# One ring of 20 buffers for ScalarE's copies, four plain column blocks in the second token block, and transposes and loads one slot earlier

## The chip, the cores and the metric

The kernel runs on one core of one Trainium2 chip. The metric is device time in microseconds (us) of that core. TensorE (PE) multiplies, VectorE (DVE) adds and takes maxima, ScalarE (ACT) mostly copies accumulators out of PSUM, GpSimd (POOL) does a few products in SBUF, and SyncE (SP) issues nearly all DMAs, one behind the other.

## The reference

A retention layer (causal attention with a decay in place of the softmax, 8 batches of 576 tokens, 8 heads of 64) is followed by a feed-forward layer whose hidden value is the maximum of three products:

```python
scores = (1 / sqrt(64)) * (q @ k^T)                 # q, k, v: (8, 8, 576, 64)
ret = scores * Dmat                                 # Dmat: gamma_h ** (i - j) for i >= j, else 0
x = (ret @ v), heads side by side                   # (4608, 512)
h = max(x @ w1, x @ w2, x @ w3)                     # w: (512, 768)
out = h @ w_out                                     # (4608, 512), float32
```

The feed-forward weights arrive in 64 bits and are converted to float32 on the chip.

## The kernel before

**Tiles.** The 4608 tokens are 36 chunks of 128 tokens; four chunks make a token block t (t = 0 to 8, 512 tokens). The 768 hidden columns are six column blocks fb of 128. The attention of a chunk is `load` (DMA), `transposes`, `decay_values` (POOL), `scores` (PE), a mask product (DVE), and, for two chunks at once, `values` (PE), whose result DVE writes to `xT`. From chunk 7 on a chunk's q and k for the transposes come in 32x32 blocks: `load` then issues 16 DMAs for `qraw`, 16 for `kxraw`, and one or two each for `kraw` and `vraw`, all on SP's queue, and the transposes are two DVE instructions (`kT`, `qT`). The buffers `qraw` and `kxraw` are two each, so that a load of chunk g + 2 waits for the transposes of chunk g.

**The order.** `ffn(t)` is a generator that hands back control 12 times per token block: nine times within the products of the hidden columns and three times within the down projection. Before each of these 12 slots the program runs the list that `steps(t + 1)` has for it: the attention of the next token block, laid out by hand. So the instructions of each engine stand in program order, and each engine works them off in that order. Small DVE jobs (sums of weights, sums of x, transposes) are put into `urgent` or `chores` and taken from there by `chore()` between matmuls; `soon(step)` puts a step into `urgent`, or runs it at once while `t = 0`, before `spread` is set.

**Hidden columns.** In t = 0 each (fb, i) is done plainly by `up_plain`: four matmuls of 128x128 by 128x512, and then ACT copies the first product (L631) or DVE takes the maximum (L630). From t = 1 on `up` does a column block with 20 products of 128x128 by 128x256 in five chains A to E, which accumulate in PSUM; sums of x (`X_SUMS`, tiles `s`) and of weights (`W_SUMS`, tiles `w` and `n`, called `weight_sums(fp)` for a pair fp of column blocks) are their operands. At certain steps of a chain `after(step)` has ACT copy the chain's present value to SBUF (L573), and DVE combines the copies (`join`, L569); the last joins give the two halves of `h`, `lo` and `hi`. The next matmul of the same chain waits for that copy. In t = 1 the column blocks 2 and 3 are still done plainly. The tiles that hold the copies exist once each: `of_a` and `of_b` with four slices each, and `a1`, `c1`, `d1`, `a7`, `b6`. PSUM has two buffers `ps_x` (chains A and B, in turn) and two `ps_y` (chains E, C, D, in turn).

**Down projection.** `downs_plain` in t = 0: four accumulators of 128x512, in the order ps_x, ps_y, ps_x, ps_y; ACT copies each to `osb` (L620), of which there are two, and SP stores it (L621). From t = 1 on `downs` does seven products per half (L419), with ACT copies (`kept`), DVE sums (`total`, L442) into the same two `osb` buffers, and stores on SP (L437).

Of the kernel before, what the change touches and what calls it, by code (L numbers as in the profile page):

```python
# [51 lines left out]
BY_PE = 7  # L52
AHEAD = 3
FILL = 224

X_SUMS = """s19 = a12 + a14, s15 = s19 - a22, s3 = a22 - a12, s10 = s3 - a13, s13 = a12 + a13, s20 = s10 + a23,
            s14 = a24 - s15, s11 = s20 + a24, s11 = a21 - s11, s7 = s11 - s13, s6 = s19 + s7,
# [5 lines left out]

PRODUCTS = """E a11 b12, E a14 b42, B s15 n5, A a22 b21, C s3 b23, B s19 b41, A s10 b32, C a13 b31, B s6 n2, A s13 b22,
              C a11 b11, B s14 n1, A s11 n4, D s7 b43, B a23 n6, A s20 b33, D s16 b13, B a21 n3, A a21 n8, A a24 n7"""
X_SUMS, W_SUMS = ([x.split() for x in text.split(",")] for text in (X_SUMS, W_SUMS))
PRODUCTS = [x.split() for x in PRODUCTS.split(",")]
WAHEAD = 6
# [3 lines left out]
def kernel(  # L72
# [30 lines left out]
    stp = ctx.enter_context(tc.tile_pool(name="stp", bufs=4))  # L103
    xpool = ctx.enter_context(tc.tile_pool(name="xpool", bufs=2))
    hpool = ctx.enter_context(tc.tile_pool(name="hpool", bufs=1))
    ppool = ctx.enter_context(tc.tile_pool(name="ppool", bufs=2))
    opool = ctx.enter_context(tc.tile_pool(name="opool", bufs=2))
    while_converting = ExitStack()
    wraw = while_converting.enter_context(tc.tile_pool(name="wraw", bufs=WAHEAD))
# [286 lines left out]
    def downs(t, h):  # L396

        def raw_hidden(r, e):
            return lambda fp: h[:, 2 * fp + e, NH * r:NH * (r + 1)]

        def summed(n):
            return lambda fp: late["S"][n][:, fp, :]

        NM = NH // P
        banks = {}
        last = t == N // NT - 1
        hS = {1: raw_hidden(0, 0), 2: raw_hidden(0, 1), 3: summed(4), 4: raw_hidden(1, 1),
              5: summed(1), 6: summed(2), 7: summed(3)}

        def bank(pool, tag, name):  # L410
            b = pool.tile([P, NM, DM // 2], FP32, tag=tag, name=name)
            both = [b[:, m, :] for m in range(NM)]
            banks[id(both)] = b
            return both

        def product(n, out, first, blocks=range(NM)):
            for fp in range(NF // 2):
                for m in blocks:
                    nc.tensor.matmul(out[m], lhsT=hS[n](fp)[:, m * P:(m + 1) * P], rhs=late["T"][n][:, fp, :],  # L419
                                     start=first and fp == 0 and (m == 0 or last and out is x),  # L420
                                     stop=fp == NF // 2 - 1, skip_group_check=True)

        def kept(name, src):
            c = ppool.tile([P, 4, NH], FP32, tag=name, name=name, bufs=1)
            if last:
                for m in range(NM):
                    nc.scalar.copy(c[:, m], src[m])
            else:
                nc.scalar.copy(c[:, 0:NM].rearrange("p m d -> p (m d)"), joined(src))
            return c  # L430

        def joined(both):
            return banks[id(both)][:].rearrange("p m d -> p (m d)")

        def store(r, c, osb, blocks=slice(None)):
            block = out[t * NT + r * NH:t * NT + (r + 1) * NH, c * (DM // 2):(c + 1) * (DM // 2)]
            nc.sync.dma_start(block.rearrange("(m p) d -> p m d", p=P)[:, blocks], osb[:, blocks])  # L437

        def total(r, c, src, others):
            osb = opool.tile([P, NM, DM // 2], FP32, tag="osb", name="osb")  # L440
            if id(src) in banks:
                nc.vector.tensor_tensor(osb[:].rearrange("p m d -> p (m d)"), joined(src),  # L442
                                        others[:, 0:NM].rearrange("p m d -> p (m d)"), op=ALU.add)
            else:
                for m in range(NM):
                    nc.vector.tensor_tensor(osb[:, m, :], src[m], others[:, m], op=ALU.add)
# [7 lines left out]
        p1 = kept("of_a", x)  # L454
# [6 lines left out]
        u2 = kept("of_a", x)  # L461
        yield
        z = bank(ps_y, "y", "dz")
        product(7, z, True)
        p7 = kept("of_b", z)
        yield
        product(5, x, False)
        total(1, 1, x, p7)
        yield
        product(4, z, False)  # L470
        total(1, 0, z, u2)
        yield
        osb = opool.tile([P, NM, DM // 2], FP32, tag="osb", name="osb")
        for blocks in ([[m] for m in range(NM)] if last else [range(NM)]):
            product(3, x, False, blocks)
            for m in blocks:
                nc.scalar.copy(osb[:, m, :], x[m])
            store(0, 1, osb, slice(blocks[0], blocks[-1] + 1))
        yield
# [75 lines left out]
    def up(t, h, fb):  # L555
# [2 lines left out]


        lo, hi = h[:, fb, 0:NH], h[:, fb, NH:NT]  # L560
        of_a = ppool.tile([P, 4, NH], FP32, tag="of_a", name="of_a", bufs=1)
        of_b = ppool.tile([P, 4, NH], FP32, tag="of_b", name="of_b", bufs=1)
        a1, c1, d1, a7, b6 = (ppool.tile([P, NH], FP32, tag=n, name=n, bufs=1)[:] for n in ("a1", "c1", "d1", "a7", "b6"))
        kept = {"C1": c1, "D1": d1, "B1": of_b[:, 1], "A1": a1, "B2": of_b[:, 0], "A2": of_a[:, 0],
                "B3": of_b[:, 2], "A3": of_a[:, 1], "B4": of_b[:, 3], "A4": of_a[:, 2], "A5": of_a[:, 3], "B6": b6, "A7": a7}
        ps = {}

        def join(out, a, b, op=ALU.add):
            nc.vector.tensor_tensor(out, a, b, op=op)  # L569

        def after(step):
            if step in kept:
                nc.scalar.copy(kept[step], ps[step[0]][:])  # L573
            if step == "B1":
                join(of_b[:, 1], ps["E"][:], of_b[:, 1])
            elif step == "A2":
                join(of_a[:, 0], of_a[:, 0], of_b[:, 0])
            elif step == "C3":
                join(of_a[:, 0], ps["C"][:], of_a[:, 0])
                join(of_a[:, 1], of_a[:, 1], of_b[:, 1])  # L580
            elif step == "A4":
                join(of_a[:, 2], of_a[:, 2], of_b[:, 2])
            elif step == "D1":
                join(of_a[:, 1:3], of_a[:, 1:3], c1.unsqueeze(1).to_broadcast([P, 2, NH]))
                join(of_a[:, 0], of_a[:, 0], of_a[:, 1], ALU.max)
            elif step == "D2":
                join(of_a[:, 2], ps["D"][:], of_a[:, 2])
                join(lo, of_a[:, 0], of_a[:, 2], ALU.max)
            elif step == "B6":
                join(of_a[:, 3], of_a[:, 3], of_b[:, 3])  # L590
                join(of_a[:, 3], of_a[:, 3], d1)
            elif step == "A7":
                join(a1, b6, a1)
                join(a1, a1, of_a[:, 3], ALU.max)
                join(hi, a7, a1, ALU.max)

        done = {}
        for chain, x, w in PRODUCTS:
# [34 lines left out]
    def ffn(t):  # L633
# [20 lines left out]
        if t == 1:  # L654
            spread.append(True)
            weight_sums(0)
            sums_of_outs()
            weight_sums(2)
            weight_sums(1)
        plain = (2, 3) if t == 1 else ()  # L660
        order = [*plain, *(fb for fb in range(NF) if fb not in plain)]
        total = sum(24 if fb in plain else len(PRODUCTS) for fb in order)
        count = parts = 0
        for n, fb in enumerate(order):
# [4 lines left out]
            for step, cost in enumerate(steps_of_one):  # L669
# [5 lines left out]
                if count * (NF // 2 * 3) >= (parts + 1) * total:  # L675
                    parts += 1
                    yield
            if order[n - 1] // 2 == fb // 2 and n % 2:
                sums_of_hidden(h, fb // 2)
        chore(len(urgent))  # L680
        for n, _ in enumerate(downs(t, h)):
            chore(4)
# [54 lines left out]
    def steps(t):  # L737
# [4 lines left out]
        def at(n, *what):  # L742
            for step, *args in what:
                if step is values:
                    if args[0][0] < NG:
                        todo[n].append(partial(values, args[0], [g for g in args[1] if g < NG]))
                elif args[0] < NG:
                    todo[n].append(partial(step, *args))

        if t == 1:  # L750
            a, b, c, d = range(CPT, 2 * CPT)
# [20 lines left out]
        return todo  # L772

    for t in range(N // NT):
# [56 lines left out]
```

## Time and profile before

| | us |
|---|---|
| median of 13 runs | 838.05 |
| lowest and highest run | 833.91, 843.52 |
| the profiled execution, its own time | 836.64 |
| its span, first to last instruction | 834.9 |
| PE busy | 789.7 (95%) |
| DVE busy | 572.1 (69%) |
| ACT busy | 301.7 (36%) |
| POOL busy | 101.2 (12%) |

All runs shown are of the same program. The views name an instruction by its line, engine, operation and tiles (output <- input); in one view the first number is the start, the second the duration, and the bracket gives the time for which the engine sat idle ahead of it and what ended that. A matmul in float32 is shown as two passes, and a row of a matmul runs longer than the distance to the next one, because matmuls overlap: PE's share of busy time is not its share of work.

### The profile page before, as it was taken

The page shows a single profiled execution, that of the slowest core. Times are in us where ns is not written, and L with a number is a line of the kernel's source. Part 1 is how long each engine was busy: PE and PEld are TensorE (multiplying, and loading weights), DVE is VectorE, ACT ScalarE, POOL GpSimd, SP SyncE. Part 2 cuts the span into 40 slices and gives each one's busy share as a digit, 9 for nine tenths or more (in the row PEclk, how much of TensorE's full clock was granted, in tenths as well). Part 3 has the DMA queues.
Part 4 walks back from the last instruction along what each step waited for, and adds up shares of the span by engine and source line. Part 5 has one row for each costly group of instructions (what it writes and reads, how often), then busy time and mean ns, then how long its engine had stood idle before and what let it go on. Part 6 is the DMA issues. An engine that isn't in the chain of part 4 may idle for free.

```text
span 834.9 us, 14056 instructions
## 1 busy us (share of the span) xinstructions
PE 789.7 (95%) x5000; PEld 627.1 (75%) x5000; DVE 572.1 (69%) x1225; ACT 301.7 (36%) x741; POOL 101.2 (12%) x124
## 2 busy tenths in 40 slices
PE   9899999969989998999899998999999989999998
PEld 7445454758878786878688786878787878788887
DVE  2997976969686828683777547682768387846672
ACT  2665531323234314441343223441344234323551
POOL 3101001311001101110101100110102010100000
PEclk9999999979999999999999999999999999999999
DMA  9996533313222331323332332223232333101001
GB/s 227 235 216 145 157 64 82 71 22 57 76 48 55 55 85 35 55 51 54 85 54 47 56 88 54 50 53 74 46 57 45 56 88 57 35 14 39 1 2 50
DMA packets 236935, 59.30 MB, mean 71 GB/s; under 512 B 217920, under 2 KB 235584, under 8 KB 236864
## 3 DMA queue, kind: packets, MB, share of 16 engines
q1 hardware_dynamic: 236432, 58.14, 32.3%
q8 instruction: 39, 0.64, 0.3%
q10 hardware_dynamic: 432, 0.27, 0.1%
q14 instruction: 32, 0.26, 0.1%
HBM read 48.89 MB, written 9.44 MB: 70 GB/s over the span
## 4 chain that ended last, share of the span: by engine, by line
PE 65%; DVE 19%; DMA 6%; SPq 5%; issue 2%; ACT 1%; POOL 0%; DVEq 0%; ACTq 0%; POOLq 0%
PE a L606 11%; PE up L627 10%; PE b L606 8%; DVE of_a L569 7%; PE dx L419 7%; PE c L606 5%; SPq L187 5%; PE s L232 5%; PE o L288 4%; PE dz L419 3%; DMA qraw<-in_q_dram 3%; DVE s L336 3%; PE down L616 2%; PE d L606 2%; DMA out_dram<-osb 2%
## 5 line engine op out<-in xcount | busy, mean ns | idle before, releaser
L573 ACT COPY of_b<-b 128x256 f32<-128x256 f32 x184 | 68.9, 374 | 177.2 <-PE b L606 146.2
L569 DVE TENSOR_TENSOR of_a<-of_a,of_b 128x256 f32<-128x256 f32 x184 | 91.7, 499 | 52.5 <-ACT of_a L573 52.3
L606 PE MATMUL a<-s,w 128*128 128x256 f32 x276 | 87.0, 397 | 16.8 <-ACT a L573 16.5
L627 PE MATMUL up<-xT,w 128*128 128x512 f32 x192 | 84.5, 595 | 0.5 <-DVE xT L176 0.5
L606 PE MATMUL b<-s,n 128*128 128x256 f32 x276 | 82.9, 382 | 1.6 <-DVE s L336 1.6
L573 ACT COPY of_a<-a 128x256 f32<-128x256 f32 x184 | 68.5, 373 | 36.3 <-PE a L606 30.3
L606 PEld LDWEIGHTS a<-s,w 128*128 128x128 f32 x276 | 49.9, 191 | 34.3 <-ACT a L573 28.7
L627 PEld LDWEIGHTS up<-xT,w 128*128 128x128 f32 x192 | 35.8, 190 | 43.5 <-issue 40.1
L606 PEld LDWEIGHTS b<-s,n 128*128 128x128 f32 x276 | 52.4, 191 | 10.3 <-ACT of_a L573 3.1
L606 PE MATMUL c<-xT,w 128*128 128x256 f32 x184 | 57.0, 392 | 0.0
L606 PE MATMUL e<-xT,w 128*128 128x256 f32 x184 | 48.0, 383 | 8.0 <-DVE w L336 8.0
L606 PE MATMUL d<-s,w 128*128 128x256 f32 x184 | 54.8, 380 | 0.0
L606 PE MATMUL b<-xT,n 128*128 128x256 f32 x184 | 54.7, 379 | 0.0
L442 DVE TENSOR_TENSOR osb<-dx,of_b 128x512 f32<-128x512 f32 x7 | 4.8, 692 | 72.1 <-PE dx L419 72.1
L573 ACT COPY a<-a 128x256 f32<-128x256 f32 x92 | 34.3, 372 | 55.0 <-DVE h L569 32.0
L261 POOL TENSOR_TENSOR state<-state,gs 128x256 f32<-128x256 f32 x24 | 18.6, 774 | 284.0 <-DVE state L260 259.2
L203 POOL TENSOR_TENSOR vd<-vraw,gk 128x512 f32<-128x512 f32 x36 | 41.1, 1142 | 63.3 <-DMA vraw<-in_v_dram 63.3
L606 PE MATMUL a<-xT,n 128*128 128x256 f32 x184 | 47.2, 379 | 0.0
L606 PEld LDWEIGHTS e<-xT,w 128*128 128x128 f32 x184 | 35.1, 191 | 13.5 <-DVE w L336 8.4
L419 PE MATMUL dx<-To,H 128*128 128x256 f32 x192 | 44.8, 383 | 0.0
L232 PEld LDWEIGHTS s<-qT,kT 64*128 64x128 f32 x576 | 37.7, 207 | 8.4 <-issue 7.1
L394 POOL TENSOR_TENSOR H<-h,H 128x256 f32<-128x256 f32 x24 | 17.8, 742 | 212.9 <-PE a L606 98.1
(116 smaller groups left out, 1479.5 us busy)
## 6 DMA issues: line engine op xcount, KB each, us to landing
bits<-in_moe_w_dram SPq DMA_DIRECT2D x36, 256.0 KB, 5.0
out_dram<-osb SPq DMA_DIRECT2D x35, 256.0 KB, 2.2
kraw<-in_k_dram SPq DMA_DIRECT2D x32, 256.0 KB, 3.0
vraw<-in_v_dram SPq DMA_DIRECT2D x32, 256.0 KB, 3.5
qraw<-in_q_dram SPq DMA_DIRECT2D x464, 16.0 KB, 1.8
kxraw<-in_k_dram SPq DMA_DIRECT2D x464, 16.0 KB, 1.8
bits<-in_moe_w_out_dram SPq DMA_DIRECT2D x6, 512.0 KB, 5.1
qraw<-in_q_dram SPq DMA_DIRECT2D x6, 256.0 KB, 4.6
```

The lines of the kernel that those rows point to most:

```text
L187: nc.sync.dma_start(t[32 * a:32 * a + 32, :, blk, :], src[b, a // 2::2, pos:pos + 32, 32 * (a % 2):32 * (a % 2) + 32].rearrange("p j i -> ...
L203: nc.gpsimd.tensor_tensor(t[:], raws.pop(("v", g))[:], gk[:].unsqueeze(2).to_broadcast([C, H, D]), op=ALU.mult)
L232: nc.tensor.matmul(s[j][:, p, :], lhsT=kT[r, p, :], rhs=qT[r, p, :], start=True, stop=True)
L261: nc.gpsimd.tensor_tensor(t[:], t[:], gs[:], op=ALU.mult)
L288: nc.tensor.matmul(o[n % 2][half(c), m, n // 2, :], lhsT=vds[g][:, h, :], rhs=sts[g][:, h % 2, h // 2, :], start=m == 0 and n < 2, stop=be ...
L336: nc.vector.tensor_tensor(dst, a, b, op=ALU.add if sign == "+" else ALU.subtract)
L394: urgent.append(lambda: (pool(s3, a11, a21, op=ALU.subtract), pool(s4, a12, s2, op=ALU.subtract)))
L419: nc.tensor.matmul(out[m], lhsT=hS[n](fp)[:, m * P:(m + 1) * P], rhs=late["T"][n][:, fp, :], start=first and fp == 0 and (m == 0 or last a ...
L569: nc.vector.tensor_tensor(out, a, b, op=op)
L573: nc.scalar.copy(kept[step], ps[step[0]][:])
L606: nc.tensor.matmul(ps[chain][:], lhsT=factor(w, fb), rhs=xS[t][x], start=n == 1, stop=ends, skip_group_check=True)
L627: nc.tensor.matmul(ps[:], lhsT=w_sb[i, fb][:, dc * P:(dc + 1) * P], rhs=xT[t][:, dc, :], start=(dc == 0), stop=(dc == NDC - 1))
```

## The change

1. **One ring.** ACT's copies of the chains and of the down projection all go to one tag, `part`, of 20 buffers of 128x256 (`PARTS`); 13 named slices and tiles are gone. A column block takes 14 of the 20 (before, 13 copies): the last value of chain D is now copied by ACT too, and DVE reads the copy where it read PSUM.
2. **The joins** stand in a table `JOINS`. C1 was added to two slices at once (a join of 128x512) ahead of a maximum; now the maximum is taken first and C1 is added to it once. So a column block has 14 joins of 128x256, before 12 of them and one of 128x512. `lo` is written after B6 and not after D2.
3. **Plain column blocks** in t = 1 are 2, 3, 4 and 5, not 2 and 3. The weight sums of pairs 1 and 2 are queued behind the plain products of their own pair, not all at the start of t = 1.
4. **Transposes and loads** of the attention stand one slot earlier, or two; a load goes through `soon`. In t = 0 this puts a whole further load into the last list.
5. In the down projection copies and sums are of 128x256 twice, not of 128x512 once.

```diff
-    ppool = ctx.enter_context(tc.tile_pool(name="ppool", bufs=2))
+    ppool = ctx.enter_context(tc.tile_pool(name="ppool", bufs=PARTS))
...
-        def kept(name, src):
-            c = ppool.tile([P, 4, NH], FP32, tag=name, name=name, bufs=1)
...
+        def kept(src):
+            both = [ppool.tile([P, NH], FP32, tag="part", name="part") for _ in range(NM)]
+            for c, x in zip(both, src):
+                nc.scalar.copy(c[:], x)
+            return both
...
-            elif step == "D1":
-                join(of_a[:, 1:3], of_a[:, 1:3], c1.unsqueeze(1).to_broadcast([P, 2, NH]))
-                join(of_a[:, 0], of_a[:, 0], of_a[:, 1], ALU.max)
-            elif step == "D2":
-                join(of_a[:, 2], ps["D"][:], of_a[:, 2])
-                join(lo, of_a[:, 0], of_a[:, 2], ALU.max)
...
+JOINS = {"B1": [("B1", ("E", "B1"), ALU.add)], "A2": [("A2", ("A2", "B2"), ALU.add)],
+         "C3": [("A2", ("C", "A2"), ALU.add)], "A3": [("A3", ("A3", "B1"), ALU.add)],
+         "A4": [("A4", ("A4", "B3"), ALU.add)],
+         "D2": [("A4", ("D2", "A4"), ALU.add), ("A3", ("A3", "A4"), ALU.max), ("A3", ("A3", "C1"), ALU.add)],
+         "B6": [("lo", ("A2", "A3"), ALU.max), ("A5", ("A5", "B4"), ALU.add), ("A5", ("A5", "D1"), ALU.add)],
+         "A7": [("A1", ("A1", "B6"), ALU.add), ("A1", ("A1", "A5"), ALU.max), ("hi", ("A1", "A7"), ALU.max)]}
...
+            if step not in ("E1", "E2", "C2", "C3", "A6", "B5"):
+                t = of[step] = ppool.tile([P, NH], FP32, tag="part", name="part")
+                nc.scalar.copy(t[:], ps[step[0]][:])
...
-            weight_sums(2)
-            weight_sums(1)
-        plain = (2, 3) if t == 1 else ()
+        plain = (2, 3, 4, 5) if t == 1 else ()
...
-            if order[n - 1] // 2 == fb // 2 and n % 2:
+            if n % 2:
                 sums_of_hidden(h, fb // 2)
+                if fb in plain:
+                    weight_sums(fb // 2)
...
-                    todo[n].append(partial(step, *args))
+                    todo[n].append(partial(soon, partial(step, *args)) if step is load else partial(step, *args))
...
-            at(11, (values, [c, d], [d, d + 1]), (load_blocks, d + 2, 3), (load, d + 2))
+            at(11, (values, [c, d], [d, d + 1]), (load_blocks, d + 2, 3), (load, d + 2),
+               (transposes, d + 1), (load, d + 3))
...
-            at(m, (keep, a), (transposes, a), (load, a + 2))
-            at(m + 1, (transposes, b), (decay_values, b))
-            at(m + 2, (scores, a), (scores, b), (load, b + 2))
+            at(m, (keep, a), (transposes, b), (decay_values, b), (load, b + 2))
+            at(m + 2, (scores, a), (scores, b))
             at(m + 4, (decay_values, a + 2))
-            at(m + 5, (values, [a, b], [b, a + 2]))
+            at(m + 5, (values, [a, b], [b, a + 2]), (transposes, a + 2), (load, a + 4))
```

Three places show what moves. The first is SP's queue where t = 0 ends: the loads of chunks 9 and 10 and the four stores of the first down projection (`out_dram<-osb`). Before:

```order
L199 DMA kraw<-in_k_dram 128x8x64
L199 DMA vraw<-in_v_dram 128x8x64
L621 DMA out_dram<-osb 128x512 x4
L187 DMA qraw<-in_q_dram 32x4x32 x16
L187 DMA kxraw<-in_k_dram 32x4x32 x16
```

Now:

```order
L207 DMA kraw<-in_k_dram 128x8x64
L207 DMA vraw<-in_v_dram 128x8x64
L195 DMA qraw<-in_q_dram 32x4x32 x16
L195 DMA kxraw<-in_k_dram 32x4x32 x16
L207 DMA kraw<-in_k_dram 128x8x64
L207 DMA vraw<-in_v_dram 128x8x64
L594 DMA out_dram<-osb 128x512 x4
```

The 34 DMAs of chunk 10 stood behind the four stores and now stand ahead of them. On SP nothing else changes places.

The second is PE in t = 1, from the second plain product of column block 3 on (`w_126` to `w_128` are the three weights, `e`, `b`, `a` accumulators of the chains). Before:

```order
L627 MATMUL up<-xT,w_127 128x512 x4
L627 MATMUL up<-xT,w_128 128x512 x4
L606 MATMUL e<-xT,w_127 128x256 x2
L606 MATMUL b<-s_1180,n_1172 128x256
L606 MATMUL a<-xT,w_126 128x256
```

Now:

```order
L600 MATMUL up<-xT,w_127 128x512 x4
L600 MATMUL up<-xT,w_128 128x512 x4
L600 MATMUL up<-xT,w_126 128x512 x4
L600 MATMUL up<-xT,w_127 128x512 x4
L600 MATMUL up<-xT,w_128 128x512 x4
L600 MATMUL up<-xT,w_126 128x512 x4
```

Two column blocks of chains (80 passes of 256 columns) gave way to two plain ones (48 passes of 512). From t = 2 on PE's order is the same as before.

The third is DVE in the first column block of a later token block, where the sums of x have just been taken (L336 before, L344 now). Before:

```order
L260 TENSOR_TENSOR state<-kv,state 128x256
L569 TENSOR_TENSOR of_a<-of_a,of_b 128x256
L260 TENSOR_TENSOR state<-kv,state 128x256
L169 STREAM_TRANSPOSE kT<-kxraw 128x512
L569 TENSOR_TENSOR of_a<-c,of_a 128x256
L569 TENSOR_TENSOR of_a<-of_a,of_b 128x256
L169 STREAM_TRANSPOSE qT<-qraw 128x512
L569 TENSOR_TENSOR of_a<-of_a,of_b 128x256
L569 TENSOR_TENSOR of_a<-of_a,c_3667 128x512
L569 TENSOR_TENSOR of_a<-of_a 128x256
```

Now:

```order
L268 TENSOR_TENSOR state<-kv,state 128x256
L559 TENSOR_TENSOR part<-part 128x256
L177 STREAM_TRANSPOSE kT<-kxraw 128x512
L559 TENSOR_TENSOR part<-part 128x256
L177 STREAM_TRANSPOSE qT<-qraw 128x512
L559 TENSOR_TENSOR part<-c,part 128x256
L559 TENSOR_TENSOR part<-part 128x256
L268 TENSOR_TENSOR state<-kv,state 128x256
```

The second update of the state went behind the first pair of transposes, the join that reads chain C's accumulator went behind the transpose of q, and the join of 128x512 is gone.

More of the change, by code (lines that the diff above doesn't have):

```diff
@@ L54 @@
 FILL = 224
+PARTS = 20
 X_SUMS = """s19 = a12 + a14, s15 = s19 - a22, s3 = a22 - a12, s10 = s3 - a13, s13 = a12 + a13, s20 = s10 + a23,
@@ L404, in downs @@
         NM = NH // P
-        banks = {}
         last = t == N // NT - 1
@@ L411, in bank @@
             b = pool.tile([P, NM, DM // 2], FP32, tag=tag, name=name)
-            both = [b[:, m, :] for m in range(NM)]
-            banks[id(both)] = b
-            return both
+            return [b[:, m, :] for m in range(NM)]
         def product(n, out, first, blocks=range(NM)):
@@ L421, in product @@
                                      stop=fp == NF // 2 - 1, skip_group_check=True)
-        def kept(name, src):
-            c = ppool.tile([P, 4, NH], FP32, tag=name, name=name, bufs=1)
[L425 to L433, printed above, removed]
+        def kept(src):
[3 more added lines that the diff above has]
+            return both
         def store(r, c, osb, blocks=slice(None)):
@@ L440, in total @@
             osb = opool.tile([P, NM, DM // 2], FP32, tag="osb", name="osb")
[L441 to L446, printed above, removed]
+            for m, o in enumerate(others):
+                nc.vector.tensor_tensor(osb[:, m, :], src[m], o[:], op=ALU.add)
             store(r, c, osb)
@@ L453, in downs @@
         product(1, x, True)
-        p1 = kept("of_a", x)
+        p1 = kept(x)
         yield
@@ L460, in downs @@
         product(6, x, False)
-        u2 = kept("of_a", x)
+        u2 = kept(x)
         yield
@@ L464, in downs @@
         product(7, z, True)
-        p7 = kept("of_b", z)
+        p7 = kept(z)
         yield
@@ L560, in up @@
         lo, hi = h[:, fb, 0:NH], h[:, fb, NH:NT]
[L561 to L566, printed above, removed]
+        ps, of = {}, {}
         def join(out, a, b, op=ALU.add):
@@ L571, in after @@
         def after(step):
[L572 to L582, printed above, removed]
-            elif step == "D1":
-                join(of_a[:, 1:3], of_a[:, 1:3], c1.unsqueeze(1).to_broadcast([P, 2, NH]))
-                join(of_a[:, 0], of_a[:, 0], of_a[:, 1], ALU.max)
-            elif step == "D2":
-                join(of_a[:, 2], ps["D"][:], of_a[:, 2])
-                join(lo, of_a[:, 0], of_a[:, 2], ALU.max)
[L589 to L595, printed above, removed]
+            if step not in ("E1", "E2", "C2", "C3", "A6", "B5"):
+                t = of[step] = ppool.tile([P, NH], FP32, tag="part", name="part")
+                nc.scalar.copy(t[:], ps[step[0]][:])
+            for out, ins, op in JOINS.get(step, ()):
+                ins = [ps[n[0]] if n in ("E", "C") else of[n] for n in ins]
+                join({"lo": lo, "hi": hi}.get(out) if out in ("lo", "hi") else of[out][:],
+                     *(x[:] for x in ins), op)
         done = {}
```

## The prediction

> **What bounds the kernel now.** I read the page's head first, then the waits grouped by who waits for whom, then the instructions in order of time where PE waits, then SP's queue.
>
> ```profile
> span 834.9 us, 14056 instructions
> PE 789.7 (95%) x5000; PEld 627.1 (75%) x5000; DVE 572.1 (69%) x1225; ACT 301.7 (36%) x741; POOL 101.2 (12%) x124
> ```
>
> PE is always needed, but its 95% hide waits, since a row of a matmul is longer than its place in the stream. The pace is read from long runs without a wait, in the chain of work that ended last:
>
> ```profile
> 102.26 13.73 PE down L616 x32
> ...
> 203.87 2.59 PE dy L419 x12
> ```
>
> A pass of 512 columns takes 13.73 / 32 = 0.429 us, one of 256 columns 2.59 / 12 = 0.216 us. A pair of the short ones is shown 0.59 us long (a row further down) where the next starts 0.43 us later, so each wait listed for PE is short by 0.16 us. The waits (us in total, times, longest):
>
> ```profile
> ACT a L573 <- DVE h L569: 32.0, 37, 1.8
> ...
> ACT of_b L573 <- DVE of_a L569: 29.2, 13, 3.5
> ...
> PE a L606 <- ACT a L573: 16.5, 17, 1.4
> ...
> PE e L606 <- DVE w L336: 8.0, 1, 8.0
> ...
> PE c L606 <- DVE of_a L569: 5.4, 5, 1.4
> ...
> PE b L606 <- ACT of_b L573: 4.8, 11, 0.7
> ...
> PE b L606 <- DVE s L336: 1.6, 4, 0.6
> ```
>
> PE waits for ACT's copies, and ACT for DVE, which is not yet done with the last column block's slices of the same tile. One such place in t = 5, in the instructions in order of time (PE, then ACT, then DVE):
>
> ```profile
> 409.52 1.03 PE L606 MATMUL e<-xT,w 128*128 128x256 f32 x4
> ...
> 412.80 0.70 PE L606 MATMUL c<-s,w 128*128 128x256 f32 x2 [1.38 <-DVE of_a L569]
> ```
>
> ```profile
> 413.62 0.37 ACT L573 COPY of_b<-b 128x256 f32<-128x256 f32 x1 [3.53 <-DVE of_a L569]
> 415.41 0.37 ACT L573 COPY a<-a 128x256 f32<-128x256 f32 x1 [1.41 <-DVE h L569]
> ```
>
> ```profile
> 414.89 0.42 DVE L569 TENSOR_TENSOR h<-a,a 128x256 f32<-128x256 f32 x1
> ```
>
> At 409.52 the second column block begins. ACT stood for 3.53 us because it could not overwrite `of_b`. The first matmul of chain C waits for DVE because it takes over chain D's PSUM buffer, which the join of D2 was still to read. DVE wrote the last half of `h` of the first column block only at 415.3, 5.8 us into the second.
>
> **The ring and the joins (items 1 and 2).** These waits are for a buffer, not for a value. With 20 buffers a copy overwrites what was kept 20 copies earlier, and a column block makes 14. The tightest case is B4 over the A1 of the block before, which DVE reads in that block's last joins: B4 is the 12th of 20 products and ends 12 x 0.43 = 5.2 us into the block, so DVE may lag 5.2 us. D2 is copied by ACT, so C waits for no join. Listed: 16.5 + 5.4 + 4.8 = 26.7 us in 17 + 5 + 11 = 33 waits; with 33 x 0.16 = 5.3 that is **-32.0**. The ends are 0 (DVE late everywhere, third rival) and -32.0; I take the latter. The lag of 5.8 us above is the longest kind (first block after the sums of x); some 0.6 us of it could be left in such a place, and DVE's wait for a store ahead of it (further down) is in it. And DVE has slack in a whole token block (busy time of PE, PEld, DVE, ACT, POOL, then the granted clock):
>
> ```profile
> 400.00:489.00 89.00, 82.38 (x565) 69.37 (x564) 59.14 (x127) 30.56 (x83) 11.21 (x13) 0.98 0.26 48
> ```
>
> DVE is busy 59 of 89 us, and its joins get no dearer: the one of 725 ns becomes a plain one (0.42 us, the DVE row above), and one more of these comes in. ACT gets one copy more per column block, 0.37 us beside 30.6 of 89.
>
> ```profile
> L569 DVE TENSOR_TENSOR of_a<-of_a,c 128x512 f32<-128x512 f32 x46 | 33.3, 725 | 1.6
> ```
>
> The splitting in the down projection (item 5) adds a copy or sum of some 0.4 us each, behind products that take 2.59 us: nothing on the path.
>
> **The slow scores.** In the chain of work three of the scores are slow, all three behind such waits (the second row is one at full pace); and in the stretches of time the granted clock, the last column but two, is down there:
>
> ```profile
> 416.53 3.41 PE s L232 x32
> ...
> 463.14 1.99 PE s L232 x32
> ...
> 509.51 3.39 PE s L232 x32
> ...
> 598.88 3.09 PE s L232 x32
> ```
>
> ```profile
> 418.00:420.00 2.00, 2.00 (x21) 1.78 (x17) 1.32 (x3) 0.00 (x0) 0.00 (x0) 0.50 0.11 15
> ```
>
> Half the clock, after waits of which the longest of PE's was 1.5 us (1.4 listed, plus 0.16), explains the difference: 3.41 + 3.39 + 3.09 - 3 x 1.99 = 3.9 us, **-3.9** if the waits go. [...]
>
> **The weight sums (item 3).** In t = 1 PE stands before the fifth column block until DVE has made its weight sums, and comes back at half pace:
>
> ```profile
> 170.34 0.59 PE L606 MATMUL e<-xT,w 128*128 128x256 f32 x2
> 178.91 1.22 PE L606 MATMUL e<-xT,w 128*128 128x256 f32 x2 [7.97 <-DVE w L336]
> ...
> 184.89 0.59 PE L606 MATMUL b<-s,n 128*128 128x256 f32 x2
> ```
>
> Now blocks 4 and 5 need no sums in t = 1, and until t = 2 there are some 90 us of PE work for the 40 sums of pairs 1 and 2: the wait goes, 7.97 + 0.16 = **-8.1**. The 14 passes from 178.91 to 184.89 took 5.98 us where 14 x 0.216 = 3.0 is the pace: **-3.0**. The two blocks cost 2 x (24 x 0.429 - 40 x 0.216) = 2 x 1.66 = **+3.3**.
>
> **The stores behind a load (item 4, t = 0).** SP, ACT, DVE and PE where t = 1 begins:
>
> ```profile
> 124.53 4.33 SPq L621 DMA_DIRECT2D out_dram<-osb  x4
> 128.95 7.52 SPq L187 DMA_DIRECT2D qraw<-in_q_dram  x16
> ...
> 144.64 0.54 SPq L199 DMA_DIRECT2D vraw<-in_v_dram  x1
> ```
>
> ```profile
> 126.73 0.59 ACT L620 COPY osb<-down 128x512 f32<-128x512 f32 x1 [1.38 <-DMA out_dram<-osb]
> ```
>
> ```profile
> 126.69 0.67 DVE L176 STREAM_TRANSPOSE qT<-qraw 128x512 f32<-128x512 f32 x1
> ```
>
> ```profile
> 126.29 13.90 PE L627 MATMUL up<-xT,w 128*128 128x512 f32 x32
> ```
>
> The third copy to `osb` waited for the first store: 126.73 - 124.53 = 2.2 us from issue to landing. That copy frees the second `ps_x` buffer, which the second plain product of t = 1 takes. Now the 34 DMAs of chunk 10 stand ahead of the stores on SP. They start when DVE has transposed chunk 8, whose buffers they take (126.69 + 0.67 = 127.4), and need 145.2 - 128.95 = 16.2 us. First store: 143.6; landed 145.8; copied 146.4. PE's first plain product ends 8 x 0.429 after 126.45 (row start 126.29 plus the 0.16), at 129.9. Stall: **+16.6**. Behind it are queued ACT's other `osb` copy and its `h` copies, but those are then in time. The stall is of the kind that ended at 178.91, so PE comes back slow: **+3.0**. Bounds: nothing is hidden, since PE has no other work in between in its order, so some 14 (loads issued faster) to 19.
>
> **Transposes and loads from t = 1 on (item 4).** The loads of a token block fill SP's queue, and the stores wait there (SP, then DVE):
>
> ```profile
> 396.32 5.32 SPq L437 DMA_DIRECT2D out_dram<-osb  x4
> 409.75 7.73 SPq L187 DMA_DIRECT2D qraw<-in_q_dram  x16
> ...
> 446.55 0.53 SPq L199 DMA_DIRECT2D vraw<-in_v_dram  x1
> 453.32 8.69 SPq L187 DMA_DIRECT2D qraw<-in_q_dram  x16
> ...
> 489.03 5.33 SPq L437 DMA_DIRECT2D out_dram<-osb  x4
> ```
>
> ```profile
> 492.70 0.69 DVE L442 TENSOR_TENSOR osb<-dz,of_a 128x512 f32<-128x512 f32 x1 [2.17 <-DMA out_dram<-osb]
> ```
>
> From store to store are 92.7 us, of which SP idles 453.32 - 447.1 = 6.2 for the transposes of the next pair. With these one slot earlier that idle time goes: SP's cycle can be 86.5 us. PE's cycle is, from the first matmuls of t = 2 to those of t = 8 in the chain of work,
>
> ```profile
> 223.47 0.86 PE e L606 x4
> ...
> 761.02 0.86 PE e L606 x4
> ```
>
> 537.6 / 6 = 89.6 us, and without the waits above 89.6 - 35.9 / 6 = 83.6. So SP has nothing to spare. A late store holds DVE at `osb<-dz`, with the sums of x behind it, and PE then waits for a sum (now 1.6 us in 4 times). The first loads of a block start when DVE is through with its transposes, which an undisturbed DVE does sooner than 13.4 us after the store; so for the other rows I take that these waits double, 1.6 + 4 x 0.16 = **+2.2**. Bounds: -2.2 (gone) and 6 x (86.5 - 83.6) = +17. The transposes of the second pair also come nearer to the landing of their loads (447 plus 2 us here): DVE may stand before them for some 3 us, within the 5.2 that the ring allows, so nothing for that.
>
> **Sum.** -32.0 - 3.9 - 8.1 - 3.0 + 3.3 + 16.6 + 3.0 + 2.2 = -21.9. Against the profiled execution's 836.64 (span 834.9 and 1.7 around it) this gives 814.7; the median of the runs is 1.4 above that execution, so I predict 816.
>
> **Rivals.** (1) SP sets the pace from t = 2 on: +17 in place of +2.2, 831. For it: 86.5 against 83.6. Against: that is the longest of SP's cycles, with two more DMAs at a batch's border.
> (2) The store's stall is hidden: 816 - 16.6 - 3.0 = 796. For it nothing but that SP may issue the loads faster; against it the order on three engines.
> (3) DVE is late, not the buffers: the next resource that PE takes from DVE, chain E's PSUM buffer, which the join of C3 has to leave, makes it wait as before. Behind C3, the 11th of 20 products, 9 more leave 9 x 0.43 = 3.9 us until the next block's E, against the 5.8 us that DVE lagged at the end of a block above. Then the 35.9 stay: 852, slower than before. It decides as soon as more than 21.9 of the 35.9 stay. Against: DVE's 59 of 89 us.
> (4) The clock falls for another reason than the waits, and the 3.9 stay: 820. [...]
>
> **Chances.** Forecast 0.60 (808 to 824), (1) 0.16, (2) 0.06, (3) 0.13, (4) 0.05. The range 803 to 832 takes in the forecast, (1) and (4). A measurement can tell some 0.5% (4.2 us) from no change: (3) I split into 0.09 slower and 0.04 within 0.5%; all else is faster.
>
> **What would show it.** Right: no wait of PE or ACT on a buffer of the ring; a wait of PE near 130 us of some 16 us that ends with ACT's `osb` copy, with the stores at 143 us; no wait for `w` near 170 us; clock 1.00 in t = 2 to 7. Wrong: PE waiting for joins at chain E or C; SP without any idle time between the stores from t = 3 on, and longer waits for `s`.

## The result, and the profile after

The changed kernel takes 806.39 us (median of 11 runs, 805.31 to 809.19); the kernel before, on the same chip, 838.24 (48 runs, 833.25 to 843.84). The ratio is 0.9624, 95% interval 0.9603 to 0.9645. The profiled execution took 808.95 us, at the upper end of the runs.

The head of the page after; the busy time of PE is 14.5 us less than before, the span 27.8 us:

```profile
span 807.1 us, 14293 instructions
...
PE 775.2 (96%) x4968; PEld 619.3 (77%) x4968; DVE 552.3 (68%) x1224; ACT 317.0 (39%) x782; POOL 100.9 (12%) x124
```

The waits after, grouped (us in total, times, longest):

```profile
PE up L600 <- ACT osb L593: 18.1, 1, 18.1
...
ACT part L564 <- DVE part L559: 8.8, 18, 0.5
...
PE b L579 <- DVE s L344: 1.9, 3, 0.7
...
PE a L579 <- ACT osb L472: 1.4, 1, 1.4
```

The 33 waits of PE for copies and joins are gone, and so is the wait for `w` near 170 us. The 18 waits of ACT put down to DVE look like waits for a ring buffer, but are none: each is 0.49 us long, the gap that a copy also has when it is put down to PE, and each copy starts within 0.1 us of the end of the product that it reads, one of them at 211.45 (210.82 + 0.59 = 211.41; ACT, then PE):

```profile
210.15 0.37 ACT L564 COPY part<-b 128x256 f32<-128x256 f32 x1 [0.49 <-PE b L579]
...
211.45 0.37 ACT L564 COPY part<-b 128x256 f32<-128x256 f32 x1 [0.49 <-DVE part L559]
```

```profile
210.82 0.59 PE L579 MATMUL b<-s,n 128*128 128x256 f32 x2
```

What is new is one row of 18.1 us. Its chain, in PE's, SP's and ACT's instructions in order of time:

```profile
127.04 3.60 PE L600 MATMUL up<-xT,w 128*128 128x512 f32 x8
148.74 11.68 PE L600 MATMUL up<-xT,w 128*128 128x512 f32 x20 [18.11 <-ACT osb L593]
```

```profile
128.14 7.67 SPq L195 DMA_DIRECT2D qraw<-in_q_dram  x16
...
143.97 0.53 SPq L207 DMA_DIRECT2D vraw<-in_v_dram  x1
144.59 5.09 SPq L594 DMA_DIRECT2D out_dram<-osb  x4
```

```profile
148.11 1.21 ACT L593 COPY osb<-down 128x512 f32<-128x512 f32 x2 [22.00 <-DMA out_dram<-osb]
```

The 34 loads run from 128.1 to 144.5, the first store starts at 144.59, ACT's third copy at 148.11, PE's second plain product at 148.74. The stretch from 400 to 489 us that was shown of before, and the stretch of the stall (busy times of PE, PEld, DVE, ACT and POOL, then the granted clock):

```profile
400.00:489.00 89.00, 88.32 (x609) 76.80 (x608) 63.55 (x148) 36.82 (x101) 11.38 (x14) 1.00 0.32 66
126.00:149.00 23.00, 4.89 (x12) 1.97 (x11) 5.51 (x13) 0.96 (x3) 1.73 (x2) 0.67 0.31 69
```

From 400 to 489 us PE is at the full clock, where it was at 0.98, and idle for 0.7 of the 89 us by its rows, where it was for 6.6; the second row shows it idle for 18 of 23 us.

### The profile page after: what moved, and what is told of

Its sections match the earlier page's. It is cut to its first block, busy times and chain, and to the rows that moved or that the text cites. A ratio compares the mean times of both kernels' runs of the same rounds, so it can differ in the third digit from the quotient of the medians.

```text
span 807.1 us, 14293 instructions
## 1 busy us (share of the span) xinstructions
PE 775.2 (96%) x4968; PEld 619.3 (77%) x4968; DVE 552.3 (68%) x1224; ACT 317.0 (39%) x782; POOL 100.9 (12%) x124
## 4 chain that ended last, share of the span: by engine, by line
PE 85%; SPq 7%; DMA 3%; DVE 3%; issue 1%; ACT 0%; DVEq 0%; ACTq 0%
PE a L579 16%; PE b L579 14%; PE up L600 13%; PE dx L424 8%; PE c L579 7%; SPq L195 5%; PE d L579 5%; PE e L579 4%; PE s L240 4%; PE o L296 4%; PE dz L424 4%; PE dy L424 2%; DMA out_dram<-osb 2%; DVE s L344 2%; PE o L309 2%; PE down L589 2%
## 5 line engine op out<-in xcount | busy, mean ns | idle before, releaser
L559 DVE TENSOR_TENSOR part<-part 128x256 f32<-128x256 f32 x440 | 198.4, 459 | 60.3 <-ACT part L564 53.3
L564 ACT COPY part<-b 128x256 f32<-128x256 f32 x220 | 82.0, 373 | 150.6 <-PE b L579 137.4
L600 PE MATMUL up<-xT,w 128*128 128x512 f32 x240 | 108.5, 609 | 18.6 <-ACT osb L593 18.1
L564 ACT COPY part<-a 128x256 f32<-128x256 f32 x264 | 98.4, 373 | 53.7 <-PE a L579 43.7
L600 PEld LDWEIGHTS up<-xT,w 128*128 128x128 f32 x240 | 45.9, 195 | 74.8 <-issue 52.1
L579 PE MATMUL a<-s,w 128*128 128x256 f32 x264 | 78.5, 379 | 0.0
L441 DVE TENSOR_TENSOR osb<-dx,part 128x256 f32<-128x256 f32 x16 | 6.1, 420 | 77.3 <-PE dx L424 70.7
L559 DVE TENSOR_TENSOR h<-part 128x256 f32<-128x256 f32 x88 | 37.4, 425 | 6.3
L424 PEld LDWEIGHTS dx<-To,H 128*128 128x128 f32 x192 | 35.9, 190 | 5.7 <-issue 1.0
L402 POOL TENSOR_TENSOR H<-h,H 128x256 f32<-128x256 f32 x24 | 18.3, 762 | 170.7 <-PE a L579 81.9
L603 DVE TENSOR_TENSOR h<-h,up 128x512 f32<-128x512 f32 x20 | 13.7, 685 | 37.4 <-PE up L600 37.2
```

Source lines behind the costliest of these rows:

```text
L402: urgent.append(lambda: (pool(s3, a11, a21, op=ALU.subtract), pool(s4, a12, s2, op=ALU.subtract)))
L564: nc.scalar.copy(t[:], ps[step[0]][:])
L579: nc.tensor.matmul(ps[chain][:], lhsT=factor(w, fb), rhs=xS[t][x], start=n == 1, stop=ends, skip_group_check=True)
L600: nc.tensor.matmul(ps[:], lhsT=w_sb[i, fb][:, dc * P:(dc + 1) * P], rhs=xT[t][:, dc, :], start=(dc == 0), stop=(dc == NDC - 1))
```

## The experiments

All times are medians in us. The kernel before had 836.1, 834.5 and 837.1 in the three groups of runs (e1, e2, e3, e5; e4, e6, e7, e9; e12 to e16), so a difference of 3 us between groups says nothing.

| kernel | what differs | us | ratio to before, interval |
|---|---|---|---|
| after | | 806.4 | 0.9624 (0.9603 to 0.9645) |
| e1 | t = 0's stores ahead of the load | 786.4 | 0.9411 (0.9363 to 0.9460) |
| e2 | ring and joins alone | 813.1 | 0.9732 (0.9690 to 0.9773) |
| e3 | after, ring of 14 | 805.9 | 0.9636 (0.9601 to 0.9671) |
| e5 | after, item 4 undone | 805.0 | 0.9623 (0.9586 to 0.9660) |
| e4 | e1, item 3 undone | 795.2 | 0.9524 (0.9479 to 0.9569) |
| e6 | after, four `osb`, ring of 14 | 782.4 | 0.9369 (0.9319 to 0.9418) |
| e7 | e1, four `osb`, ring of 14 | 782.7 | 0.9383 (0.9348 to 0.9418) |
| e9 | e1, D2 read in PSUM | 787.5 | 0.9436 (0.9396 to 0.9476) |
| e12 | e5, four `osb`, ring of 14 | 781.8 | 0.9315 (0.9271 to 0.9359) |
| e13 | e7, ring of 10 | 782.4 | 0.9321 (0.9270 to 0.9372) |
| e14 | before, four `osb` | 828.5 | 0.9872 (0.9827 to 0.9918) |
| e16 | e7, 14 named buffers | 836.4 | 0.9985 (0.9956 to 1.0014) |

### The stall at the start of t = 1: e1 and e6

e1 takes only chunk 10's load out of the last list of t = 0:

```diff
-               (transposes, d + 1), (load, d + 3))
+               (transposes, d + 1))
...
+            if t == 2 and n == 0:
+                at(m, (load, a + 2))
```

> The changed kernel, but the load of chunk 10 is issued behind the four stores of t = 0 again, as in the kernel before; all else as changed. Theory (the stores behind 34 DMAs hold ACT's copies to osb, and these hold PE's second plain product): the wait of 18.3 us near 130 us and the 14 half-rate passes behind it (2.9 us) go, 806.4 - 21.2 = 785 us. Rival (PE would wait there for something else, DVE's weight sums of pair 0, once the stores are on time): 795 to 806 us, with a new wait of PE for w in t = 1.

Measured 786.4, 20.0 less than the changed kernel. In SP's order the stores are back ahead of the load, and PE's first four plain products (eight passes each) run through in one row:

```profile
125.12 4.39 SPq L594 DMA_DIRECT2D out_dram<-osb  x4
129.60 7.55 SPq L195 DMA_DIRECT2D qraw<-in_q_dram  x16
```

```profile
126.89 13.90 PE L600 MATMUL up<-xT,w 128*128 128x512 f32 x32
```

e6 leaves the changed kernel's order alone and gives `osb` four buffers (the ring is cut to 14 to make room, which by e3 costs nothing):

```diff
-PARTS = 20
+PARTS = 14
...
-    opool = ctx.enter_context(tc.tile_pool(name="opool", bufs=2))
+    opool = ctx.enter_context(tc.tile_pool(name="opool", bufs=4))
```

> The changed kernel with its order untouched (the load of chunk 10 ahead of t = 0's stores), but four buffers for osb in place of two, and 14 ring buffers to make room (which alone gave 805.9). Theory (PE's 18 us near 149 us are one chain: third osb copy waits for the first store, the store waits behind 34 DMAs on SP, and PE waits for that copy's PSUM buffer): with an osb buffer free the copy needs no store, so PE does not stand, though the stores still start near 144.6 us: 806 - 21 = 785, and up to 4 less where the waits of later token blocks for osb go too. Rival (the DMAs of loads and stores themselves hold PE, or h or the weights are late there): most of the 18 us stay, 800 to 806.

Measured 782.4. The stores (the last row of SP's) are as late as ever, behind the last DMA of the load, but ACT's third copy no longer waits for the first of them, and PE has its accumulator:

```profile
146.41 1.41 SPq L207 DMA_DIRECT2D vraw<-in_v_dram  x1
147.92 2.04 SPq L594 DMA_DIRECT2D out_dram<-osb  x4
```

```profile
128.82 0.59 ACT L593 COPY osb<-down 128x512 f32<-128x512 f32 x1 [0.27 <-PE down L589]
```

```profile
129.47 13.90 PE L600 MATMUL up<-xT,w 128*128 128x512 f32 x32
```

So the chain is store, `osb`, copy, PSUM buffer, PE, and either end of it can be cut. It is not the traffic of the DMAs.

### From t = 2 on: e2, e5 and e12

e2 is the kernel before with items 1, 2 and 5 alone: ring, joins, and the split copies of the down projection; plain blocks 2 and 3 and the old lists.

> The kernel before with items 1, 2 and 5 alone (ring of 20, the new joins, copies of 128x256); plain blocks 2 and 3, and all transposes and loads where they were. Theory (buffers, not values, were waited for): all waits for ACT's copies and for the joins go, 33 us and the slow scores' 4 to 5 us, 838.2 - 37 = 801 us or somewhat less; the wait of 8 us for w in t = 1 stays. Rival (DVE is late, PE waits at chain E or C instead): 830 us or more. Rival (what was gained came with the earlier transposes): 815 to 830 us.

Measured 813.1: the theory missed by 12 us, and the second rival was nearer. The ring's waits are all gone, but a new one stands at the start of five token blocks (grouped waits of e2, then SP, ACT and PE at one place):

```profile
PE a L579 <- ACT osb L472: 15.7, 5, 3.9
```

```profile
480.33 5.40 SPq L436 DMA_DIRECT2D out_dram<-osb  x4
```

```profile
484.68 0.65 ACT L472 COPY osb<-dx 128x256 f32<-128x256 f32 x2 [15.24 <-DMA out_dram<-osb]
```

```profile
485.38 1.22 PE L579 MATMUL a<-xT,w 128*128 128x256 f32 x2 [3.70 <-ACT osb L472]
```

The store starts at 480.33, when SP is through with the loads; it landed before 484.68, when ACT's copy into `osb` could start; that copy frees the `ps_x` buffer which chain A takes. It is the chain of t = 1 once more. Without the ring's waits PE arrives earlier than SP.

e5 is the changed kernel with item 4 undone everywhere:

```diff
...
-               (transposes, d + 1), (load, d + 3))
...
-            at(m, (keep, a), (transposes, b), (decay_values, b), (load, b + 2))
-            at(m + 2, (scores, a), (scores, b))
+            at(m, (keep, a), (transposes, a), (load, a + 2))
+            at(m + 1, (transposes, b), (decay_values, b))
+            at(m + 2, (scores, a), (scores, b), (load, b + 2))
...
-            at(m + 5, (values, [a, b], [b, a + 2]), (transposes, a + 2), (load, a + 4))
+            at(m + 5, (values, [a, b], [b, a + 2]))
```

> The changed kernel with item 4 undone everywhere: transposes and loads at the places of the kernel before (so the stores of t = 0 are first on SP again too); ring and four plain blocks as changed. Theory (item 4 costs its stall of 21.2 us in t = 1 and is worth little otherwise, since the loads still land in time): 785 to 790 us, like the first of these runs, with the waits for s at most 4 us more than there. Rival (earlier transposes and loads carry part of the gain from t = 2 on, since SP would set the pace without them): 795 us or more.

Measured 805.0, where 785 was the theory's: the rival was right. It has no stall in t = 1, but six waits like e2's:

```profile
PE a L579 <- ACT osb L472: 15.0, 6, 3.4
```

Against e1, which differs in the lists alone, e5 is 18.6 us longer. In the two, SP, ACT and PE work off the same order; only DVE's transposes, which free the buffers for the loads, stand elsewhere. So item 4 costs 20 us in t = 1 and gives back 18.6 from t = 2 on, which is why the changed kernel with it (806.4) and without it (805.0) cannot be told apart.

e12 is e5 with four `osb` buffers and a ring of 14.

> The ring and the four plain blocks with item 4 undone (805.0 with two osb buffers), now with four buffers for osb and 14 for the ring. Theory (from t = 2 on, too, the earlier transposes and loads only cured a wait of DVE and ACT for an osb buffer, whose store stands behind the loads on SP): with osb buffers free the order of loads and transposes is worth nothing, 782 to 785, and the stores still stand behind the loads. Rival (the transposes themselves are late in the old order, so that scores or sums come late whatever the stores do): PE's waits at the starts of the token blocks stay, some 3 us in each of six, 797 to 805.

Measured 781.8, as good as e6 and e7. Its stores still stand behind a load on SP,

```profile
457.96 0.53 SPq L207 DMA_DIRECT2D vraw<-in_v_dram  x1
458.58 2.65 SPq L436 DMA_DIRECT2D out_dram<-osb  x4
```

and PE waits for neither `osb` nor `s` any more. With two `osb` buffers the places of transposes and loads are worth some 20 us either way, in t = 1 by SP's order and from t = 2 on by the time at which the loads begin; with four they are worth nothing.

### Both cures at once: e7

e7 has e1's order and e6's buffers.

> t = 0's stores ahead of the load and four osb buffers, with 14 ring buffers. Theory: in the kernel with the stores ahead alone (786.4) the only waits left from t = 2 on are those that end with an osb copy or a sum behind it, some 3 to 4 us, and these go: 782 to 784. Rival (both edits take away the same thing, and the remaining waits are for the transposes or for loads): 786, no difference.

Measured 782.7; e1 had 786.4 in another group, and the intervals of the two ratios overlap, so the times do not settle it. The waits do: the small ones behind `osb` and `s` are gone, and a stretch of 80 us in the middle shows no idle time of PE at all:

```profile
400.00:480.00 80.00, 80.00 (x572) 70.05 (x571) 57.45 (x131) 32.43 (x89) 11.10 (x13) 1.00 0.32 65
```

The four kernels with four `osb` buffers and a ring (e6, e7, e12, e13) lie within 1 us. Any of them beats both kernels of this study.

### What of the ring matters: e3, e13, e16, e14 and e9

e3 is the changed kernel with `PARTS = 14`, e13 is e7 with `PARTS = 10`.

> The changed kernel with a ring of 14 buffers, the number that one column block takes, so that each copy goes over the same chain step of the block before (until the down projection shifts it). Theory (the depth of the ring is what frees ACT): A1's copy waits again for the last joins of the block before, which read that buffer; 17 waits of some 1.1 us came from this before, so 20 to 33 us come back, 826 to 838 us. Rival (D2's copy on ACT and slices of their own were enough, depth does not matter): 806 to 810 us.

> The same kernel (782.7) with 10 shared buffers. At the end of D2 the values still wanted are A1, C1, A2, A3, B4, A4, D1, D2 and A5, nine, and DVE is some 3.7 us late, in which ACT makes two or three more copies. Theory (the pool needs what is alive plus DVE's lag, about 12): PE waits again, by 0.4 to 1 us in each of some 44 column blocks: 798 to 825. Rival (ten are enough, since DVE frees most of them early in a block): 783 to 786.

Neither number of buffers made a difference (805.9 and 782.4): both theories fell. In e13 a few copies do wait for a buffer, but never long enough for PE to notice. Of the 56 waits put down to DVE most are again the ordinary gap; nine copies start more than 0.1 us behind the end of their product, by 0.8 us at most:

```profile
ACT part L564 <- DVE part L559: 26.4, 56, 0.8
```

The addresses in the built program say why: the pool does not go round. A copy gets a buffer that was freed before. With 14 buffers (e3, e7) B1 of a block takes over what B2 of the block before had, A1 what B1 had, and the A1 of the block before, which its last joins read, is overwritten only by B6 or A7, the 18th and 20th of the 20 products, or behind a down projection by B4, the 12th.

e16 is e7 with the same 14 buffers, but one for each step's name (the copies of the down projection are given four of these names):

```diff
...
-                t = of[step] = ppool.tile([P, NH], FP32, tag="part", name="part")
+                t = of[step] = ppool.tile([P, NH], FP32, tag=step, name="part", bufs=1)
```

> The kernel with t = 0's stores ahead of the load, four osb buffers and 14 buffers for the copies (782.7), but the 14 are no longer a pool: each copy has a buffer of its own name, as before, so that a copy overwrites the same step's copy of the column block before; in the down projection the copies go over A2, A3 and B2, B1. The joins of the table stay. Theory (sharing is what matters, not the number of buffers nor the joins): the ring waits return, 33 us by starts, and some half-rate passes behind them, 815 to 820. Rival (the joins and the copy of D2 made DVE early enough): 783 to 788.

Measured 836.4: 53.7 more than e7, and all that the change had gained is gone. The waits, then one column block on PE, ACT and DVE:

```profile
PE a L579 <- ACT part L564: 41.3, 35, 2.3
...
ACT part L564 <- DVE h L559: 58.9, 36, 2.8
```

```profile
412.06 1.03 PE L579 MATMUL e<-xT,w 128*128 128x256 f32 x4
...
415.80 0.70 PE L579 MATMUL a<-s,w 128*128 128x256 f32 x2 [0.99 <-ACT part L564]
416.34 0.59 PE L579 MATMUL c<-xT,w 128*128 128x256 f32 x2
```

```profile
415.38 0.37 ACT L564 COPY part<-a 128x256 f32<-128x256 f32 x1 [1.45 <-DVE h L559]
```

```profile
414.86 0.42 DVE L559 TENSOR_TENSOR h<-part 128x256 f32<-128x256 f32 x1
```

DVE ends the last join of a block 3.2 us into the next (415.28 after 412.06). A1's copy, due at 413.9, where the product that it reads ends, overwrites the A1 which that join reads, so ACT stands 1.45 us and PE behind it 0.99. PE has such a wait in 35 of the 44 column blocks. Listed they are 41.3 us; with 0.16 for what the list leaves out of each, and 0.10 for the pair behind it, that is some 51, and the spans of e16 and e7 lie 50.9 apart (832.2 and 781.3).

The theory's 33 us were too few because it took the waits of before. There DVE ended the last join 2.1 to 2.4 us into the next block in most column blocks, and 5.8 at most. With the new table it is 3.2 us at the least, in e16 and in e7 alike: nine joins stand behind D2, where seven did. So the table makes DVE later, named buffers meet that each time, and sharing hides it. What the old joins would give with shared buffers was not run.

e14 is the kernel before with four `osb` buffers and nothing else.

> The kernel before with nothing changed but four buffers for osb in place of two. Theory (ACT stands on the named copies because each is overwritten one column block after it was written, and DVE is 3 to 6 us late in every column block, not only behind a store): the 33 waits on copies and joins stay, and only the waits for s behind a late store go, 2 to 6 us of some 835. Rival (DVE is late because a store holds it at osb, and what it loses there makes it late in the column blocks behind): a good part of the 33 us goes, 800 to 820.

Measured 828.5, 1.3% or 8.7 us less than the kernel before in that group, where the theory had 2 to 6. The waits on copies and joins:

```profile
PE a L606 <- ACT a L573: 15.5, 16, 1.1
...
PE b L606 <- ACT of_b L573: 4.5, 10, 0.6
...
PE c L606 <- DVE of_a L569: 1.9, 4, 0.7
```

These are 21.9 us in 30, where the kernel before had 26.7 in 33. So the theory holds for the most part: by these two profiles about a fifth of the waits went with the late stores, and four fifths stay as long as the copies have names.

e9 is e1 with D2 not copied; DVE reads chain D's accumulator.

> The kernel with t = 0's stores ahead of the load (786.4 us), but chain D's end not kept by ACT: DVE reads it in its PSUM buffer again, in one of its joins. Theory: chain C, which takes over that buffer, waits for the join again; before there were 5.4 us listed in 5 such waits (6.2 with 0.16 each), with half-rate passes behind some: 791 to 795. Rival (those waits came from DVE's being late because ACT was held up on the ring, and go with the ring alone): 786, or a little less, since ACT has a copy less.

Measured 787.5 against 786.4, not told apart, and PE waits for no join at chain C. The 14th copy is not needed; the waits at chain C came from a late DVE and went with the rest.

### The weight sums: e4

e4 is e1 with plain blocks 2 and 3 only, and the sums where they were.

> The kernel with t = 0's stores ahead of the load (786.4 us), with item 3 undone: only blocks (2, 3) are plain in t = 1, and DVE makes all weight sums where it made them before. Theory (the wait for the sums is a matter of DVE's place in its order, whatever the ring does): PE stands some 8 us for w before the fifth column block of t = 1 and comes back at half rate, and the two plain blocks cost nothing any more: 786.4 + 8.1 + 3.0 - 3.3 = 794. Rival (DVE, no longer held up by ring buffers and joins in t = 1, has the sums ready in time): the wait is below 3 us and the kernel gains by the cheaper blocks, 783 to 786.

Measured 795.2: 8.8 more than e1. The wait is back at its place and with nearly its length, though ACT and DVE are no longer held by names:

```profile
178.61 1.22 PE L579 MATMUL e<-xT,w 128*128 128x256 f32 x2 [7.59 <-DVE w L344]
```

## Why the prediction was right, and where it was off

The forecast was 816 with 803 to 832; it came out at 806.4, on the side forecast and inside the range. Its likeliest case happened: store stall there, ring waits gone, SP not the bound. That the sum came so near is in part luck, as two of the steps below show.

From span to span the sum said -21.9 and the traces say -27.8. By PE's starts, over the pace of 0.429 and 0.216 us a pass:

| term | predicted | measured |
|---|---|---|
| ring and joins, 33 waits (measured with five too short for the list) | -32.0 | -33.1 |
| starts that are 0.10 us late: some 52 fewer, most of these behind waits | not counted | -5.2 |
| half-rate scores and passes behind them | -3.9 | -5.2 |
| wait for the weight sums, and restart | -8.1 - 3.0 | -8.1 - 2.9 |
| two plain blocks | +3.3 | +3.3 |
| store stall in t = 1 | +16.6 | +18.3 |
| restart behind it | +3.0 | +2.9 |
| waits for `s` and `osb` from t = 2 on | +2.2 | +1.8 |
| sum | -21.9 | -28.2 |

The sum passes the spans' difference by 0.4 us: in the first 31 us, where loads landed later (PE waited 3.5 us for `kraw`, before 2.8), the changed kernel lost 0.75, and the rest are differences too small to list. Two terms were mis-sized. The pair behind a wait was priced like any other, 0.59 us long and 0.43 to the next; it is shown 0.70 long with 0.54 to the next (415.80 to 416.34 above), and the same 0.70 stood in the row at 412.80 that the prediction quoted. And the landing of the store took 3.5 us (144.59 to 148.11), not 2.2. The 2.2 came from a store ahead of which SP had stood idle for 4 us; right behind loads, stores took 3.0 to 4.1 us in the kernel before too, and the prediction's own rows at 489.03 and 492.70 show one of 3.7. (The figures that it gives for the stall add up to 16.5, not 16.6; and of the 3.53 us at 413.62 that ACT stood, 0.9 lay ahead of the end of the product, so the copy was 2.6 us late. Neither changes the sum.) Of the 9.6 us between 816 and 806.4, 5.9 are the difference between the forecast and the measured change of the span; the rest is from run to run: the profiled execution of before lay 1.4 under its median, that of after lies 2.6 over it.

**The ring's reason was wrong, though its size was right.** The step that failed is "a copy overwrites what was kept 20 copies earlier", with the 5.2 us of lag worked out from it. By the addresses a copy takes a buffer freed before, not the one of 20 copies earlier, and by e3 and e13 neither 20 nor 14 matters; ten do. What matters is that a copy needn't go over its own name (e16).

**SP's term came out for another reason than given.** "I take that these waits double" priced the earlier loads as a side cost of +2.2, against a bound of +17 which was the first rival. That rival is real: with the ring and without item 4, e2 and e5 show 15 to 16 us of such waits, and from token block to token block their stores come 84 to 87 us apart in the middle of the kernel, about the rival's 86.5. In the changed kernel they come 82 to 85 us apart there, with SP idle for 9 to 11 us of that. Item 4 is what removed it, by 18.6 us, and the prediction counted for item 4 only what it costs. The two errors, a cost not seen and a cure not seen, cancelled; that is luck.

**The store stall** was right in place and chain, and within 1.7 us in size: PE stands to 148.7, ending with ACT's `osb` copy, the stores at 144.6 (143 was forecast). The second rival, that it is hidden, needs a free `osb` buffer (e6).

**DVE's lag** (third rival): no wait of PE at chain E or C after, and only 1.9 us for `s`. Yet DVE is later than before in most column blocks, 3.2 to 4.8 us behind PE at a block's end where it was 2.1 to 5.8; apart from those 1.9 us no listed wait of PE comes of it.

**The clock** (fourth rival): 1.00 from 222 to 755 us (t = 2 to 7) once the waits were gone, before 0.99 with three falls to 0.50, so the slow scores did hang on them.

## What to carry to other kernels

Give temporaries that one engine writes and a lagging engine reads one shared pool, not a buffer per name: a pool of ten hid a lag that cost 54 us with 14 buffers named one by one. Before reordering loads and stores on one issuing queue, ask what the store releases: here the buffer it frees stood two steps ahead of PE, and two more such buffers made each of the three orders tried equally good. And when the largest wait is taken away, work out which engine or queue PE then reaches too early, since part of the gain goes there (here 15 to 16 us of 33).

## What the runs showed of the hardware

Whether PE comes back slow from a wait did not follow from the wait's length. PE's rows after two waits, in e2 and in e5 (each starts with the wait's end):

```profile
398.33 0.70 PE L579 MATMUL a<-xT,w 128*128 128x256 f32 x2 [3.46 <-ACT osb L472]
398.87 0.59 PE L579 MATMUL c<-s,w 128*128 128x256 f32 x2
```

```profile
390.86 1.22 PE L579 MATMUL a<-xT,w 128*128 128x256 f32 x2 [2.41 <-ACT osb L472]
391.87 1.06 PE L579 MATMUL c<-s,w 128*128 128x256 f32 x2
```

After 3.46 us listed, in e2, PE is at full pace, the second pair 0.59 us long; after 2.41 us, in e5, the second is 1.06 us long and starts 1.01 us behind the first, not 0.54. The granted clock was 0.50 in e5 and 1.00 in e2 (busy times as above, then the granted clock; e5, then e2):

```profile
390.88:394.29 3.41, 3.41 (x8) 2.78 (x9) 3.31 (x10) 1.32 (x4) 0.00 (x0) 0.50 0.44 154
```

```profile
396.61:400.02 3.41, 1.69 (x8) 1.48 (x9) 2.97 (x9) 1.76 (x6) 0.00 (x0) 1.00 0.44 156
```

Nor did the wait's releaser decide it: in e2 itself PE came back slow after 3.70 us that ended with the same copy (1.22 us, the row at 485.38 above). In the kernel before, the granted clock fell to 0.50 at 416.8, 509.0 and 597.7 us, behind two or three waits of 0.55 to 1.39 us listed each. What decides whether the clock falls was not shown.
